# Scratch in DRAM laid out anew: token numbers 64 bytes apart, rows of x of 2112 bytes, rows of columns 320 bytes longer

## The chip, the core and the metric

The kernel runs on one core of a Trainium2 chip. The metric is the device time of one execution in microseconds. A core has five engines that run side by side, each with its own queue of instructions: TensorE (PE, with its weight loads as PEld), VectorE (DVE), ScalarE (ACT), GpSimd (POOL) and SyncE (SP), which here issues most DMAs. DMAs of all queues run on the core's 16 DMA engines, and the profile lists the fetches of the engines' own instructions among them, as queues of kind "instruction".

## The reference, cut to what matters

Three layers over 3072 tokens (4 sequences of 768) of 512 values:

```
scores = q @ k.T / 8; keep the first 4 keys and the last 128;  a = softmax(scores);  x = a @ v     # 8 heads of 64
logits = x @ w_gate + bias[modality];  e = argmax(logits);  gate = softmax(logits)[e]              # 8 experts
y[token] = gate * (relu(x[token] @ w1[e]) @ w2[e])                                                 # one expert a token
h = y @ w_in;  out = (h * sigmoid(1.702 * h)) @ w_out                                              # 512 -> 2048 -> 512
```

All inputs are float32. Which tokens an expert has is known on the chip only, so tokens are sorted there: rows of x go to DRAM, are gathered by expert, and the result goes to the right rows of the output at the end.

## The kernel before

**Attention** (up to about 240 us) runs over 24 tiles of 128 tokens; the order of its steps is a table of due times. At the end of each tile `norm` (L313 to L321) writes 128 rows of x to the scratch `xd`: the row of a token has 512 values and, behind them, one more place for its gate weight, 513 floats or 2052 bytes in all. The gate weights are made by `gate` (L791) in two batches, for tiles 0 to 15 while attention runs (L803 to L806) and for tiles 16 to 23 during routing: a sum, an addition, a reciprocal, and a DMA that puts one 4-byte word into each row. The DMA issues stand on SP's queue in the program's order.

**Routing** (about 244 to 262 us, mostly VectorE) sorts the tokens by expert and leaves lists of token numbers in `perm`, 128 to a column. One expert is chosen early from the first 2048 tokens, and its first pair of tiles is worked on while the rest is routed.

**Expert stage.** A pair is two tiles of 128 tokens of one expert (`pair`, and for the first one the loop over `ADV`). For each, POOL gathers the rows of x with their weights into the two tiles `xg` by an indirect DMA (`gather`, L1039), ACT multiplies by the weight (`weigh`, L1139), PE transposes, and then for eight chunks f of the hidden layer PE does 12 up-matmuls (`up`, L1166) and 12 down-matmuls (`down_pair`, L1181); ACT and DVE split each result into two parts between them. `yout` (L1240) evicts the pair's result into `ys` (L1245 on ACT and L1247 on DVE), columns by token, and `columns` (L1234) issues two DMAs for each place:

```
q.dma_start(out=m["y" + nm][:, :, bass.ds(at, n)]..., in_=ys[:, :, 0:n])      # L1237: 4 x 128 rows of n columns
q.dma_start(out=m["t" + nm][bass.ds(at, n)]..., in_=perm[:, j : j + n // P])   # L1238: the n token numbers
```

`yb` holds the columns of all tokens in sorted order (row pitch 12288 bytes), `ya` those of the first 1024 again (4096 bytes), and `tb` and `ta` their token numbers, 4 bytes each. The first pair goes to `ya`, the next three to `ya` and `yb`, the others to `yb`. Behind these DMAs on SP's queue stand weight chunks: of the next expert (`load_chunk`, L1095 and L1096), and of the last layer (`cload`, L1335 and L1337), which DVE and POOL convert. What is left over of an expert, up to 128 tokens, is done **alone** (`one`; up-matmuls L1478, down-matmuls L1487, loads under the branch of L1492): one tile, one matmul where a pair has three, weights read in place, and the next such expert's chunks are loaded as chunks come free; here POOL issues the y and token DMAs.

**Last layer** (from about 602 us). Twelve turns, two halves of the hidden layer by six groups of 512 tokens. `x2load` (L1468) reads the next group's columns and, in the second half, its token numbers into `oidx` (L1470) one turn ahead. The results are scattered to the output's rows by indirect DMAs (L1575).

Of the kernel before, what the change touches and what calls it, by code (L numbers as in the profile page):

```python
# [6 lines left out]
F32 = mybir.dt.float32  # L7
# [3 lines left out]
I32 = mybir.dt.int32  # L11
U32 = mybir.dt.uint32
AF = mybir.ActivationFunctionType
# [4 lines left out]
P = 128  # L18
B, H, S, D = 4, 8, 768, 64
NT = S // P  # L20
T = B * NT
E = 8
DM = H * D
# [767 lines left out]
def gate(tc, cst, pool, xd):  # L791

    nc = tc.nc
    V = nc.vector
    sm = pool.tile([P, T], F32, name="g_sm")
    d = cst["d"]

    def exps(a, b):
        V.tensor_tensor(out=d[:, a:b], in0=d[:, a:b], in1=cst["mx"][:, a:b].unsqueeze(2).broadcast_to([P, b - a, E]), op=ALU.subtract)
        nc.scalar.activation(out=d[:, a:b], in_=d[:, a:b], func=AF.Exp)  # L800

    def weights(a, b):
        V.tensor_reduce(out=sm[:, a:b], in_=d[:, a:b], op=ALU.add, axis=AX.X)  # L803
        V.tensor_scalar(out=sm[:, a:b], in0=sm[:, a:b], scalar1=1e-9, scalar2=None, op0=ALU.add)
        V.reciprocal(sm[:, a:b], sm[:, a:b])
        nc.sync.dma_start(out=xd[a * P : b * P, DM:].rearrange("(t p) o -> p (t o)", p=P), in_=sm[:, a:b])  # L806

    return exps, weights

# [200 lines left out]
NU = 16  # L1010
ADV = [(0, 7), (4, 8), (5, 1), (12, 0), (12, 2), (11, 5)]
F = 1024
CH = F // P
NG_ = T * P // 512


def whole(tc, q, k, v, n_sink, window, mid, wg, mb, w1, w2, w_in, w_out, out):
    nc = tc.nc
    w_in, w_out = w_in.bitcast(U32), w_out.bitcast(U32)
    with ExitStack() as ctx:  # L1020
        dp = ctx.enter_context(tc.tile_pool(name="dram", bufs=1, space=bass.MemoryType.DRAM))
        keep = ctx.enter_context(tc.tile_pool(name="keep", bufs=1))
        rp = ctx.enter_context(tc.tile_pool(name="raw", bufs=1))
        m = {}
        m["xd"] = dp.tile([T * P, DM + 1], F32, name="xd")

        for nm, n in (("a", 8 * P), ("b", T * P)):
            m["y" + nm] = dp.tile([4, P, n], F32, name="y" + nm)
            m["t" + nm] = dp.tile([n, 1], I32, name="t" + nm)
        m["yp"] = dp.tile([T * P, DM], F32, name="yp")  # L1030
        raw = [rp.tile([P, F], F32, name=f"raw{i}") for i in range(CH)]
        perm = keep.tile([P, NC], I32, name="perm")
        gp = ctx.enter_context(tc.tile_pool(name="xg", bufs=1, side="right"))
        xg = [gp.tile([P, DM + 1], F32, name=f"xg{i}") for i in range(2)]

        def gather(i, j):

# [61 lines left out]
def layers(tc, cst, ctx, c1, m, raw, keep, perm, gates, xg, gather, load, w_in, w_out, out):  # L1099
# [5 lines left out]
    nc = tc.nc  # L1105
    V, A, G = nc.vector, nc.scalar, nc.gpsimd
# [6 lines left out]
    def parts(p, nm, a, b):  # L1113
        return [(p.tile([P, F], F32R, name=f"{nm}h{i}"), p.tile([P, F], F32R, name=f"{nm}l{i}")) for i in range(a, b)]

# [20 lines left out]
    def weigh(i):  # L1136

        x = xg[i][:, 0:DM]
        A.activation(out=x, in_=x, func=AF.Copy, scale=xg[i][:, DM:])  # L1139

    def gather_alone(s):

# [3 lines left out]
    def trans_alone(s):  # L1146

        x = xs[s % 2]
        A.activation(out=x[:, 0:DM], in_=x[:, 0:DM], func=AF.Copy, scale=x[:, DM:])
        trans([x[:, 0:DM]], [(x, k) for k in range(4)])  # L1150

    def xtrans(u, blocks=range(2)):
# [45 lines left out]
    while (what := (yield)) is not None:  # L1198
        n = int(what[-1]) if what[-1].isdigit() else 0
        if what == "scores":  # L1200
            rp = pool("x", side="right")
            xt += [(rp.tile([P, F], F32R, name=f"xh{i}"), rp.tile([P, F], F32R, name=f"xl{i}")) for i in range(2)]
            hx += [rp.tile([P, 512], F32R, name=f"h{i}") for i in range(3)]
# [30 lines left out]
    def columns(q, places, n, j):  # L1234

        for nm, at in places:
            q.dma_start(out=m["y" + nm][:, :, bass.ds(at, n)].rearrange("k p c -> p k c"), in_=ys[:, :, 0:n])  # L1237
            q.dma_start(out=m["t" + nm][bass.ds(at, n)].rearrange("(i p) o -> p (i o)", p=P), in_=perm[:, j : j + n // P])  # L1238

    def yout(u, q=nc.sync):  # L1240

# [39 lines left out]
    cd, wb, xs = [], [], []  # L1281
# [25 lines left out]
    def left3():  # L1307
        nonlocal ca, cw
        c1.close()
        rp = pool("cd", side="right")  # L1310
        cd.extend(rp.tile([P, 2 * DM], F32, name=f"cd{i}") for i in range(2))
        wb.extend(parts(pool("wb", side="right"), "wb", 0, CH))
        tp = pool("moe")
        ca = tp.tile([P, 512], U32, name="ca")
        cw = tp.tile([P, 512], F32, name="cw")
        tp = pool("xs", c3)
        xs.extend(tp.tile([P, DM + 1], F32, name=f"xs{i}") for i in range(2))
        fresh[0] = flag(1, 1, (ET.SP,))
        expert[2] = expert_of(0, 2)
        with tc.If(fresh[0] != 0):  # L1320
            for c in range(CH):
                load(expert[2], c)
        ahead(1)
        cload(0)
        cload(1)
# [136 lines left out]
    oidx = keep.tile([P, T], I32, name="oidx")  # L1462

    def x2load(g, index=False):

        nm, a = ("b", 512 * g - 256) if g else ("a", 0)
        for i, x in enumerate(cd):
            nc.sync.dma_start(out=x.rearrange("p (k c) -> p k c", k=2), in_=m["y" + nm][2 * i : 2 * i + 2, :, a : a + 512].rearrange("k p c -> p k c"))  # L1468
        if index:
            nc.sync.dma_start(out=oidx[:, 4 * g : 4 * g + 4], in_=m["t" + nm][a : a + 512].rearrange("(t p) o -> p (t o)", p=P))  # L1470


    def first_alone(s, f):
# [68 lines left out]
    tp = pool("mlp")  # L1542
# [98 lines left out]
```

## Time and profile before

| | |
|---|---|
| time, median of 3 runs | 1136.49 us (1130.78 to 1139.29) |
| the profiled execution's own time | 1139.11 us, its span 1137.5 us |
| busy: PE, PEld | 1082.0 us (95%), 916.0 us (81%) |
| busy: DVE, ACT, POOL | 553.5 us (49%), 418.1 us (37%), 242.8 us (21%) |
| mean granted clock of PE | 0.975 |
| DMA | 172115 packets, 108.49 MB, 95 GB/s mean |
| packets under 512 bytes | 118000 |

Busy time is a mean over stages with different limits. [...] A timeline row has the start, the duration in us, engine, line, operation, and in square brackets the idle time ahead with what ended it; "issue" means that the profile shows nothing that the engine waited for.

### The profile page before, as it was taken

The page shows a single profiled execution, that of the slowest core. Times are in us where ns is not written, and L with a number is a line of the kernel's source. Part 1 is how long each engine was busy: PE and PEld are TensorE (multiplying, and loading weights), DVE is VectorE, ACT ScalarE, POOL GpSimd, SP SyncE. Part 2 cuts the span into 40 slices and gives each one's busy share as a digit, 9 for nine tenths or more (in the row PEclk, how much of TensorE's full clock was granted, in tenths as well). Part 3 has the DMA queues.
Part 4 walks back from the last instruction along what each step waited for, and adds up shares of the span by engine and source line. Part 5 has one row for each costly group of instructions (what it writes and reads, how often), then busy time and mean ns, then how long its engine had stood idle before and what let it go on. Part 6 is the DMA issues. An engine that isn't in the chain of part 4 may idle for free. (4 is left out here: it accounts for less than half of the span.)

```text
span 1137.5 us, 18802 instructions
## 1 busy us (share of the span) xinstructions
PE 1082.0 (95%) x6625; PEld 916.0 (81%) x6625; DVE 553.5 (49%) x1385; ACT 418.1 (37%) x1026; POOL 242.8 (21%) x397
## 2 busy tenths in 40 slices
PE   7999999888999999999869999999999999999996
PEld 4676766578998999999867888888888888888885
DVE  3776677785544484522102566656533334234242
ACT  4887887643222342222112323323323222223221
POOL 2523131452332233211100222222210011011011
PEclk8999999988988999999979999999999999999999
DMA  6667677642777865435666313112023023033010
GB/s 119 130 114 134 127 118 108 147 78 62 125 90 100 195 129 104 57 57 162 106 166 179 111 41 126 45 67 75 2 74 111 10 102 112 1 111 136 13 38 37
DMA packets 172115, 108.49 MB, mean 95 GB/s; under 512 B 118000, under 2 KB 149744, under 8 KB 171984
## 3 DMA queue, kind: packets, MB, share of 16 engines
q1 hardware_dynamic: 167184, 91.43, 38.3%
q0 software_dynamic: 4800, 15.49, 4.3%
q8 instruction: 60, 0.98, 0.4%
q14 instruction: 71, 0.58, 0.2%
HBM read 79.61 MB, written 27.29 MB: 94 GB/s over the span
## 5 line engine op out<-in xcount | busy, mean ns | idle before, releaser
L1166 PE MATMUL pu<-xh,wah 128*128 128x256 f32 (+1 forms) x576 | 187.3, 325 | 0.0
L1166 PE MATMUL pu<-xh,wal 128*128 128x256 f32 (+1 forms) x576 | 185.8, 323 | 0.4 <-DVEq L1275 0.4
L1166 PE MATMUL pu<-xl,wah 128*128 128x256 f32 (+1 forms) x576 | 185.7, 322 | 0.0
L1551 DVE TENSOR_TENSOR raw<-pu,raw 128x512 f32<-128x512 f32 x96 | 66.3, 691 | 244.8 <-ACT raw L1550 210.4
L1550 ACT ACTIVATE raw<-pu 128x512 f32<-128x512 f32 x96 | 57.4, 598 | 291.9 <-PE pu L1166 286.8
L1181 PE MATMUL pa<-h,wah 128*128 128x256 f32 x768 | 158.4, 288 | 5.1 <-issue 5.1
L1181 PEld LDWEIGHTS pa<-h,wah 128*128 128x128 f32 x768 | 130.3, 197 | 4.1 <-issue 4.1
L1166 PEld LDWEIGHTS pu<-xh,wal 128*128 128x128 f32 x576 | 112.2, 195 | 8.4 <-DVEq L1275 0.6
L1166 PEld LDWEIGHTS pu<-xh,wah 128*128 128x128 f32 x576 | 112.2, 195 | 8.3 <-issue 0.4
L1166 PEld LDWEIGHTS pu<-xl,wah 128*128 128x128 f32 x576 | 112.1, 195 | 7.5
L1181 PE MATMUL pa<-h,wal 128*128 128x256 f32 x384 | 110.6, 288 | 1.9 <-issue 1.9
L1189 ACT ACTIVATE h<-pu 128x256 fp32r<-128x256 f32 x96 | 36.9, 384 | 200.0 <-PE pu L1166 177.0
L1192 DVE SCALAR_TENSOR_TENSOR h<-pu,h 128x256 fp32r<-128x256 f32 x96 | 40.5, 422 | 125.2 <-ACT h L1189 64.5
L202 DVE CUSTOM_DVE_ANT_0 sc<-s,m 128x260 f32<-128x260 f32 (+1 forms) x192 | 73.1, 399 | 52.8 <-PE s L194 46.9
L211 ACT ACTIVATE pn<-sc,mx 128x260 f32<-128x260 f32 (+1 forms) x192 | 92.0, 483 | 5.2 <-DVE mx L202 4.7
L1118 ACT ACTIVATE h<-raw 128x512 fp32r<-128x512 f32 x96 | 60.7, 632 | 77.7 <-DVE raw L1551 77.7
L1181 PEld LDWEIGHTS pa<-h,wal 128*128 128x128 f32 x384 | 75.8, 197 | 3.4 <-issue 3.4
L1173 PE MATMUL pa<-wah,h 128*128 128x512 f32 x216 | 76.3, 389 | 0.0
L1173 PE MATMUL pa<-wbh,h 128*128 128x512 f32 x216 | 76.3, 389 | 0.0
L1166 PE MATMUL pu<-xh,wbh 128*128 128x512 f32 x192 | 74.8, 390 | 1.0 <-ACT y L1489 1.0
L1166 PE MATMUL pu<-xh,wbl 128*128 128x512 f32 x192 | 74.8, 390 | 0.0
L1166 PE MATMUL pu<-xl,wbh 128*128 128x512 f32 x192 | 74.8, 390 | 0.0
(327 smaller groups left out, 2067.8 us busy)
## 6 DMA issues: line engine op xcount, KB each, us to landing
raw<-in_moe_w_dram SPq DMA_DIRECT2D x64, 256.0 KB
cd<-yb SPq DMA_DIRECT2D x20, 512.0 KB
xd<-xe SPq DMA_DIRECT2D x24, 256.0 KB
raw<-yp SPq DMA_DIRECT2D x12, 512.0 KB
qn<-in_q_dram SPq DMA_DIRECT2D x22, 256.0 KB
kn<-in_k_dram SPq DMA_DIRECT2D x22, 256.0 KB
vn<-in_v_dram SPq DMA_DIRECT2D x22, 256.0 KB
yb<-y SPq DMA_DIRECT2D x10, 512.0 KB
```

The source lines that it names most:

```text
L202: nc.vector.tensor_tensor_reduce(out=sc[:, :n], in0=ps[:, :n], in1=m[:, :n], scale=1.0, scalar=3.0e38, op0=ALU.add, op1=ALU.min, accum_out=mx)
L211: nc.scalar.activation(out=pn[t][:, h, :n], in_=sc[:, :n], func=AF.Exp, scale=-1.0, bias=mx, accum_out=sums[t][:, h : h + 1])
L1118: A.activation(out=hi, in_=x, func=AF.Copy)
L1166: nc.tensor.matmul(ps[:, 0:n], w[a][:, s], cols(x, b, k), start=(k == 0 and i == 0), stop=(k == 3 and i == 2))
L1173: nc.tensor.matmul(acc, h[a][:, s], w[b][:, 512:], start=(f == 0 and j == 0), stop=(f == last and j == 2))
L1181: nc.tensor.matmul(acc[:, i % 2 * 256 : i % 2 * 256 + 256], wa[f][a][:, s], h[b], start=(f == 0 and i % 2 == 0 and j == 0), stop=(f == CH ...
L1189: A.activation(out=hi, in_=ps, func=AF.Relu)
L1192: V.scalar_tensor_tensor(out=lo, in0=ps, scalar=0.0, in1=hi.bitcast(F32), op0=ALU.max, op1=ALU.subtract)
L1550: A.activation(out=s, in_=ps, func=AF.Sigmoid, scale=1.702)
L1551: V.tensor_tensor(out=s, in0=ps, in1=s, op=ALU.mult)
```

## The change

`xd` gets rows of 528 floats (2112 bytes, 33 times 64), and the tiles that rows are gathered into (`xg`, `xs`) grow alike. The reciprocal writes each weight 16 times, into a new tile `g_sl`, and the DMA puts all 16 (64 bytes) behind the 512 values; the readers use the first. `ta` and `tb` have 16 places of 4 bytes for each token, of which the first is written and read. The rows of `ya` and `yb` are 80 floats (320 bytes) longer than their columns. No arithmetic changes.

```diff
--- before.py
+++ after.py
@@ -793,6 +793,7 @@
     nc = tc.nc
     V = nc.vector
     sm = pool.tile([P, T], F32, name="g_sm")
+    sl = pool.tile([P, T, LINE], F32, name="g_sl")
     d = cst["d"]
 
     def exps(a, b):
@@ -802,8 +803,8 @@
     def weights(a, b):
         V.tensor_reduce(out=sm[:, a:b], in_=d[:, a:b], op=ALU.add, axis=AX.X)
         V.tensor_scalar(out=sm[:, a:b], in0=sm[:, a:b], scalar1=1e-9, scalar2=None, op0=ALU.add)
-        V.reciprocal(sm[:, a:b], sm[:, a:b])
-        nc.sync.dma_start(out=xd[a * P : b * P, DM:].rearrange("(t p) o -> p (t o)", p=P), in_=sm[:, a:b])
+        V.reciprocal(sl[:, a:b], sm[:, a:b].unsqueeze(2).broadcast_to([P, b - a, LINE]))
+        nc.sync.dma_start(out=xd[a * P : b * P, DM:].rearrange("(t p) o -> p t o", p=P), in_=sl[:, a:b])
 
     return exps, weights
 
@@ -1010,6 +1011,9 @@
 NU = 16
 ADV = [(0, 7), (4, 8), (5, 1), (12, 0), (12, 2), (11, 5)]
 F = 1024
+LINE = 16
+PAD = 5 * LINE
+XD = DM + LINE
 CH = F // P
 NG_ = T * P // 512
 
@@ -1022,16 +1026,16 @@
         keep = ctx.enter_context(tc.tile_pool(name="keep", bufs=1))
         rp = ctx.enter_context(tc.tile_pool(name="raw", bufs=1))
         m = {}
-        m["xd"] = dp.tile([T * P, DM + 1], F32, name="xd")
+        m["xd"] = dp.tile([T * P, XD], F32, name="xd")
 
         for nm, n in (("a", 8 * P), ("b", T * P)):
-            m["y" + nm] = dp.tile([4, P, n], F32, name="y" + nm)
-            m["t" + nm] = dp.tile([n, 1], I32, name="t" + nm)
+            m["y" + nm] = dp.tile([4, P, n + PAD], F32, name="y" + nm)
+            m["t" + nm] = dp.tile([n, LINE], I32, name="t" + nm)
         m["yp"] = dp.tile([T * P, DM], F32, name="yp")
         raw = [rp.tile([P, F], F32, name=f"raw{i}") for i in range(CH)]
         perm = keep.tile([P, NC], I32, name="perm")
         gp = ctx.enter_context(tc.tile_pool(name="xg", bufs=1, side="right"))
-        xg = [gp.tile([P, DM + 1], F32, name=f"xg{i}") for i in range(2)]
+        xg = [gp.tile([P, XD], F32, name=f"xg{i}") for i in range(2)]
 
         def gather(i, j):
 
@@ -1136,7 +1140,7 @@
     def weigh(i):
 
         x = xg[i][:, 0:DM]
-        A.activation(out=x, in_=x, func=AF.Copy, scale=xg[i][:, DM:])
+        A.activation(out=x, in_=x, func=AF.Copy, scale=xg[i][:, DM : DM + 1])
 
     def gather_alone(s):
 
@@ -1146,7 +1150,7 @@
     def trans_alone(s):
 
         x = xs[s % 2]
-        A.activation(out=x[:, 0:DM], in_=x[:, 0:DM], func=AF.Copy, scale=x[:, DM:])
+        A.activation(out=x[:, 0:DM], in_=x[:, 0:DM], func=AF.Copy, scale=x[:, DM : DM + 1])
         trans([x[:, 0:DM]], [(x, k) for k in range(4)])
 
     def xtrans(u, blocks=range(2)):
@@ -1235,7 +1239,7 @@
 
         for nm, at in places:
             q.dma_start(out=m["y" + nm][:, :, bass.ds(at, n)].rearrange("k p c -> p k c"), in_=ys[:, :, 0:n])
-            q.dma_start(out=m["t" + nm][bass.ds(at, n)].rearrange("(i p) o -> p (i o)", p=P), in_=perm[:, j : j + n // P])
+            q.dma_start(out=m["t" + nm][bass.ds(at, n), 0:1].rearrange("(i p) o -> p (i o)", p=P), in_=perm[:, j : j + n // P])
 
     def yout(u, q=nc.sync):
 
@@ -1314,7 +1318,7 @@
         ca = tp.tile([P, 512], U32, name="ca")
         cw = tp.tile([P, 512], F32, name="cw")
         tp = pool("xs", c3)
-        xs.extend(tp.tile([P, DM + 1], F32, name=f"xs{i}") for i in range(2))
+        xs.extend(tp.tile([P, XD], F32, name=f"xs{i}") for i in range(2))
         fresh[0] = flag(1, 1, (ET.SP,))
         expert[2] = expert_of(0, 2)
         with tc.If(fresh[0] != 0):
@@ -1467,7 +1471,7 @@
         for i, x in enumerate(cd):
             nc.sync.dma_start(out=x.rearrange("p (k c) -> p k c", k=2), in_=m["y" + nm][2 * i : 2 * i + 2, :, a : a + 512].rearrange("k p c -> p k c"))
         if index:
-            nc.sync.dma_start(out=oidx[:, 4 * g : 4 * g + 4], in_=m["t" + nm][a : a + 512].rearrange("(t p) o -> p (t o)", p=P))
+            nc.sync.dma_start(out=oidx[:, 4 * g : 4 * g + 4], in_=m["t" + nm][a : a + 512, 0:1].rearrange("(t p) o -> p (t o)", p=P))
 
 
     def first_alone(s, f):
```

On VectorE's queue one instruction has another size in each batch of weights. In the second batch, in the routing, there stood before (the names are the tiles, `r_` those of the routing):

```order
L803 TENSOR_REDUCE g_sm<-pk_d 128x8
L804 TENSOR_SCALAR g_sm<-g_sm 128x8
L805 RECIPROCAL g_sm<-g_sm 128x8
L860 TENSOR_SCALAR r_pn<-r_n 128x8
L862 TENSOR_SCALAR r_pn<-r_pn 128x8
```

and now stands:

```order
L804 TENSOR_REDUCE g_sm<-pk_d 128x8
L805 TENSOR_SCALAR g_sm<-g_sm 128x8
L806 RECIPROCAL g_sl<-g_sm 128x128
L861 TENSOR_SCALAR r_pn<-r_n 128x8
L863 TENSOR_SCALAR r_pn<-r_pn 128x8
```

Nothing moved; the reciprocal has 128 values a partition in place of 8, and 256 in place of 16 in the first batch.

On SP's queue, the DMAs of a pair's result with the computation of their places, before (pair 2, counted from 0):

```order
L1237 REGISTER_ALU
L1237 DMA yb<-y 128x4x256
L1238 REGISTER_ALU
L1238 DMA tb<-perm 128x2x1
L1237 REGISTER_ALU
L1237 DMA ya<-y 128x4x256
L1238 REGISTER_ALU
L1238 DMA ta<-perm 128x2x1
```

and now:

```order
L1241 REGISTER_ALU
L1241 DMA yb<-y 128x4x256
L1242 ISA
L1242 DMA tb<-perm 128x2x1
L1241 REGISTER_ALU
L1241 DMA ya<-y 128x4x256
L1242 ISA
L1242 DMA ta<-perm 128x2x1
```

The DMAs are as many and in the same order; ahead of a token write another instruction computes its place. In later pairs one such instruction is added.

## Rows read from the trace of the kernel before

**Rows 1.** The page, its first part, and PE in its 40 slices.

```profile
PE 1082.0 (95%) x6625; PEld 916.0 (81%) x6625; DVE 553.5 (49%) x1385; ACT 418.1 (37%) x1026; POOL 242.8 (21%) x397
...
PE   7999999888999999999869999999999999999996
```

**Rows 2.** Windows between evictions of y; pair 1 first; columns named above.

```profile
core 0: us, PE busy (x) PEld busy (x) DVE busy (x) ACT busy (x) POOL busy (x), PEclk, DMA share, GB/s
297.99:328.62 30.63, 26.33 (x202) 26.23 (x201) 12.25 (x27) 5.97 (x13) 9.02 (x9) 0.89 0.69 96
328.62:359.01 30.39, 27.78 (x206) 27.04 (x205) 11.96 (x26) 7.30 (x15) 9.04 (x9) 0.89 0.73 96
359.01:387.62 28.61, 26.37 (x206) 25.98 (x205) 11.96 (x26) 7.30 (x16) 8.00 (x8) 0.94 1.03 152
387.62:411.53 23.91, 23.91 (x202) 23.91 (x201) 18.75 (x30) 11.89 (x19) 9.64 (x8) 1.00 0.73 195
```

**Rows 3.** Timeline of SP: the token write of a later pair.

```profile
437.62 0.39 SPq L1238 DMA_DIRECT2D tb<-perm  x1
```

**Rows 4.** Windows of 1 us behind that token write.

```profile
439.00:440.00 1.00, 1.00 (x11) 1.00 (x10) 0.00 (x0) 0.21 (x1) 0.91 (x2) 1.00 0.65 177
...
442.00:443.00 1.00, 1.00 (x11) 1.00 (x10) 0.01 (x1) 0.64 (x2) 0.00 (x0) 1.00 0.00 0
...
445.00:446.00 1.00, 1.00 (x11) 1.00 (x10) 0.90 (x3) 0.00 (x0) 0.80 (x1) 1.00 1.05 45
...
449.00:450.00 1.00, 1.00 (x11) 1.00 (x10) 0.93 (x3) 0.00 (x1) 0.00 (x0) 1.00 0.96 349
```

**Rows 5.** Window of 1 us in pair 0's write of y.

```profile
274.00:275.00 1.00, 1.00 (x11) 1.00 (x10) 0.97 (x8) 0.42 (x2) 0.00 (x0) 1.00 0.99 336
```

**Rows 6.** Timeline of PE in pair 2, first and last of three gaps.

```profile
312.85 0.28 PE L1181 MATMUL pa<-h,wah 128*128 128x256 f32 x1 [2.15 <-issue]
...
315.64 0.37 PE L1181 MATMUL pa<-h,wah 128*128 128x256 f32 x1 [1.03 <-issue]
```

**Rows 7.** DMA queues (packets, MB, share) in 197:201, 245:248, 252:254.

```profile
q8 instruction: 1, 0.02, 9.2%
...
q1 hardware_dynamic: 1040, 0.00, 15.6%
...
q8 instruction: 1, 0.02, 2.7%
```

**Rows 8.** Windows in the stretch of experts that run alone.

```profile
554.00:602.00 48.00, 34.20 (x260) 33.04 (x260) 2.92 (x5) 8.61 (x24) 3.99 (x5) 0.86 0.65 134
...
562.00:563.00 1.00, 1.00 (x11) 1.00 (x10) 0.00 (x0) 0.28 (x1) 0.00 (x0) 1.00 1.12 12
...
587.00:588.00 1.00, 0.00 (x0) 0.00 (x0) 0.00 (x0) 0.30 (x1) 0.00 (x0) 1.00 0.17 27
```

**Rows 9.** Timeline of PE in that stretch, its two longest gaps.

```profile
572.31 1.01 PE L1478 MATMUL pu<-xs,raw 128*128 128x128 f32 x3 [5.34 <-DMA raw<-in_moe_w_dram]
...
592.37 1.01 PE L1478 MATMUL pu<-xs,raw 128*128 128x128 f32 x3 [5.76 <-SPq L1492]
```

**Rows 10.** Chain that ended last (start, us, what): one chunk at full clock.

```profile
596.15 1.09 PE pu L1478 x8
597.24 0.89 PE pa L1487 x8
```

**Rows 11.** The tile of gate weights: reciprocals and DMAs (duration ns min/median/max).

```profile
L805 DVE RECIPROCAL g_sm<-g_sm x2: 202/228/253, 193.1 to 245.5; 128x16 f32<-128x16 f32 x1, 128x8 f32<-128x8 f32 x1
L806 SPq DMA_DIRECT2D xd<-g_sm x2: 382/386/389, 193.4 to 245.7; - x2
```

**Rows 12.** Timeline of PE in the opening: waits for the first gathered tiles.

```profile
226.25 0.33 PE L1130 MATMUL pu<-ident,xg 128*128 128x128 f32 x1 [2.74 <-ACT xg L1139]
...
228.25 1.75 PE L1130 MATMUL pu<-ident,xg 128*128 128x128 f32 x7 [1.67 <-ACT xg L1139]
```

**Rows 13.** Window in the routing.

```profile
249.00:252.00 3.00, 3.00 (x27) 3.00 (x27) 3.00 (x11) 1.34 (x2) 1.46 (x2) 1.00 0.00 0
```

## The prediction

> **What bounds the kernel now.** I read the page's first part, then the windows stage by stage, and only then single instructions. TensorE is busy for 1082.0 of 1137.5 us [rows 1], so no engine beside it can give much; what a change of memory layout can give lies in the 55 us in which TensorE stands still and in the time its clock is lowered after standing still. The windows by pair of the expert stage show where that is [rows 2]: from one eviction of y to the next a pair of 256 tokens takes 30.63, 30.39 and 28.61 us three times running, and 23.91 us in the fourth. The matmuls are the same (202, and 206 in two, where four transposes are added), but the granted clock is 0.89, 0.89 and 0.94 in place of 1.00 and TensorE is not busy all the time. The 23.91 is what the work costs; the rest is stall.
>
> Why it stalls is seen one level down. After each eviction the kernel issues y and then the token numbers: for the later pair shown, 128x2 words of 4 bytes to adjacent places at 437.62 [rows 3]. By the microsecond [rows 4], the queue moves 177 GB/s in the slice in which these words go (439 to 440), then 0 in 442 to 443 and 45 in 445 to 446, with a weight chunk waiting behind them, and 349 again from 449 on: about 9 us of jam behind 1 KB. It isn't y that jams: in 274 to 275, while the last of pair 0's y goes and a gather beside it, the rate is 336 GB/s [rows 5]. In the three slow pairs y and the numbers go out twice, to two places, and there TensorE stops in the middle of an accumulation, matmul by matmul, with no releaser (three gaps; the first and the last of them in [rows 6]): nothing but its next instructions can be late, and these come over the same DMA engines (a code packet of 0.02 MB takes 9.2% of 16 engines over 4 us, which is 5.9 us, when it meets short writes, and 2.7% over 2 us, 0.9 us, when it does not [rows 7]). [...]
>
> The second place is the stretch of the experts that run alone: 48 us for 260 matmuls, clock 0.86 [rows 8], with gaps of 5.34 and 5.76 us before matmuls that wait for weights [rows 9]. The rate falls to 12 and 27 GB/s in it [rows 8], behind token writes again. The rest, from 602 us to the end, is steady matmul work with its x2 and index loads a whole turn ahead; nothing in the change reaches it.
>
> **The change part by part.**
>
> *Token numbers 64 bytes apart.* As many writes of 4 bytes, no two within 64 bytes. Is the jam made by their number or by their adjacency? The trace holds the other case: the gate weights, 4 bytes each and 2052 bytes apart. Their 2048 words are issued at 193.4 [rows 11], and the code packet of the window from 197 on takes its 5.9 us, to 203 [rows 7]: about 9 us for 2048, 4.4 ns each. The second batch (1040 packets after 245.7) is gone when a code packet of 0.9 us passes after 252 [rows 7]: under 5 us, at most 5 ns each. The adjacent 256 cost 9 us, 35 ns each. So adjacency costs eight times, and 256 apart should cost 256 x 5 ns, some 1.3 us. Ends: 0 and 9 us a batch; I take 1.3, the row of like instructions. The worth, then:
> - Pairs: 6.72 + (6.48 - 0.5) + (4.70 - 0.5) = 16.9 us over 23.91 [rows 2], the 0.5 for the four transposes that two of them add (four at the 0.12 us a matmul of these rows). A jam of 2.6 us for two batches is shorter than the 9 us that the later pairs ride out without loss. I take 16.0; ends 0 and 16.9.
> - Experts alone: eight up-matmuls take 1.09 and eight down-matmuls 0.89 us at full clock [rows 10], so two experts of eight chunks take 2 x 8 x 1.98 = 31.7, with the transposes 32.2; the stretch took 48, so 15.8 is stall and low clock. What is late next is the weights themselves: 4 MB an expert, which at the 177 to 349 GB/s outside the jam of rows 4 needs 12 to 24 us, beside 16 us of matmuls. So I leave some 3 us of it: 12.5; ends 0 and 15.8.
>
> *Rows of x from 64-byte places, weight 16 times.* A row was 2052 bytes, so its 256-byte pieces began 4 bytes further on in each row; now 2112. The gathers move 3% more. Where they matter is the opening: TensorE waits 2.74 and 1.67 us for two gathered tiles, 4.4 in all [rows 12], issued right beside a write of x. With the edges of the pieces whole, the write should clear sooner. That is inferred, not shown; ends 0 and 4.4, I take 3.0. In the attention stage the same writes stand among the loads, but TensorE's slices read 9 there from the second on [rows 1], with no idle time to give back, so I cost it at nothing; its cover is the two-tile lead of the loads.
>
> *The reciprocal.* It now writes 256 and 128 values in place of 16 and 8. 16 took 0.25 and 8 took 0.20 us [rows 11]: 6.4 ns a value, so 256 take 1.79 and 128 take 0.97: +1.5 and +0.8. The second lies where VectorE is busy throughout (3.00 of 3 us [rows 13]) and everything waits for the routing: its 0.8 counts in full. The first lies in attention, where VectorE has gaps: ends 0 and 1.5, I take 0.7. Together +1.5. The gathers that need the weights come long after.
>
> *Rows of columns 320 bytes longer.* y already goes at 336 GB/s [rows 5]; nothing to gain, and its reads are ahead of need. Zero; a cost would be hidden by the turn of lead. The instruction that replaces a register operation on SP ahead of a token write, and one added in later pairs, stand in a queue that waits for y anyway: zero.
>
> Sum against the profiled execution's 1139.1 us: -16.0 - 12.5 - 3.0 + 1.5 = -30.0, so **1109 us**. That execution lies 2.6 us above the median of 1136.49, and the runs spread over 8.5 us; since stalls are what I remove, I count from the execution that shows them.
>
> [...] In the rows, 4-byte writes 2052 bytes apart cost an eighth of adjacent ones. [...] The weights in rows 7 and the tokens in rows 4, of one length and two spacings, speak against length alone, but no row shows 64 bytes.
>
> **The rivals.**
> - *The short write itself is the cost (no change).* Every 4-byte write would still be slow, and 64 bytes too little distance: the unit that serialises may be wider, or the 16 KB that 256 tokens now cover may still meet at one place. Then the jams stay at 9 us and only the reciprocals count: 1139.1 + 1.5, down to 1136 where rows of x help: 1136 to 1142. For it: no row has a spacing between 4 and 2052 bytes. Against: whatever the unit's width, sixteen times fewer tokens share one. 12%.
> - *The jam goes, the stall half stays.* The pairs run free, but the lone experts become bound by their weight loads, or code still comes late in one pair: half of 28.5 is given back, 1117 to 1128. For it: in that stretch the loads are issued only as chunks come free. Against: a chunk comes free three chunks after its use, five before its place is read again, which is 5 x 1.98 = 10 us of lead. 9%.
> - *The other side: each place costs what 64 bytes cost now.* 256 tokens fill 16 pieces of 64 bytes and take 9 us, 0.56 us a piece. If the piece is what costs, and not the words in it, 256 pieces cost more than now. It decides from where a jam is longer than the 9 us that the later pairs ride out; at 18 us the eight later pairs would lose what the first three lose, 5.6 on average, and the lone stretch 9 twice: 1139 + 45 + 18 = 1202 us, and more for longer jams. Against: 2048 weights, each in a piece of its own, cleared in 9 us [rows 7]. 5%.
>
> **How the numbers follow.** The forecast holds 74%: 1100 to 1117, from the ends of its terms (-16.9 - 15.8 - 4.4 + 0.8 gives 1103, and a little for stalls too small for a row; half the lone stretch kept and nothing from the opening gives 1117). With the half case up to 1128 the range **1100 to 1128** leaves out the other two cases and a little at its edges, 2 in 10. A measurement can't tell less than about 1% from no change, 11 us, so faster means below 1125: the forecast and most of the half case, 0.80; within 1%: no change and the rest of it, 0.14; slower 0.06.
>
> **What would show it.** Right: all pairs at 23.9 to 24.5 us with clock 1.00; over 200 GB/s within 2 us of a token write wherever something is queued behind it; the stretch of lone experts at 34 to 37 us; the gaps without a releaser gone; reciprocals of about 1.8 and 1.0 us. Wrong: the rate falls to tens of GB/s for 8 us behind the tokens as before (no change), or for longer (slower); weight waits of several us among lone experts with no jam ahead of them (half). If the gathers of the opening still end late while the tokens run free, the term of 3.0 was wrong and the rest stands.

## The result, and the profile after

The changed kernel takes **1103.47 us** (median of 4 runs, 1102.95 to 1104.96), the kernel before in the same comparison 1135.45 us (4 runs, 1130.78 to 1139.29): ratio 0.9729, 95% interval 0.9699 to 0.9758. The forecast was 1109 us, 1100 to 1128. The profiled execution took 1102.95 us (span 1101.4), 36.2 us less than the one the prediction counted from.

In what follows a line of the changed kernel has a number one to four higher than before: the up-matmuls are L1170, the y and token DMAs L1241 and L1242.

The first part of the page, and PE in its 40 slices:

```profile
PE 1068.0 (97%) x6625; PEld 904.5 (82%) x6625; DVE 553.7 (50%) x1385; ACT 418.2 (38%) x1026; POOL 241.9 (22%) x397
...
PE   6999999978999999999989999999999999999996
```

As many matmuls, 14 us less busy time (fewer of them at half clock, PEclk 0.50, as before from 343.9 to 350.7 us; the mean granted clock is 0.989, against 0.975), and of 36 us in all the rest is time in which TensorE stood still. The windows between evictions of y, with the columns of [rows 2], show where (in brackets the number of instructions; PEclk is the granted clock of PE as a share of full speed; the DMA share, of the 16 DMA engines, can pass 1 in a short window, since a packet's whole time is put where it began); the last row is the stretch of the experts that run alone, from the last pair's eviction to the last lone one's:

```profile
294.67:318.58 23.91, 23.91 (x202) 23.91 (x201) 11.95 (x26) 5.97 (x14) 8.98 (x9) 1.00 0.40 124
318.58:343.00 24.42, 24.42 (x206) 24.34 (x205) 11.95 (x26) 7.29 (x15) 8.99 (x9) 1.00 0.39 120
343.00:367.54 24.54, 24.54 (x206) 24.37 (x205) 11.96 (x26) 7.30 (x16) 7.95 (x8) 1.00 0.77 238
367.54:391.45 23.91, 23.91 (x202) 23.91 (x201) 18.75 (x30) 11.88 (x19) 9.60 (x8) 1.00 0.42 134
532.06:565.24 33.18, 30.38 (x266) 29.63 (x264) 3.46 (x5) 9.21 (x25) 3.99 (x5) 1.00 0.66 195
```

The three doubled pairs take what the fourth always took; the four added transposes are the 0.5 us that was allowed for. Between the same evictions the lone stretch took 48.65 us before. The whole difference by the times of the evictions of y:

| stretch | before | after | difference | forecast |
|---|---|---|---|---|
| start to pair 0's y | 270.00 | 266.92 | -3.08 | -3.0 + 1.5, opening and reciprocals |
| first pair after it | 27.99 | 27.75 | -0.24 | 0 |
| three doubled pairs | 89.64 | 72.87 | -16.77 | -16.0 |
| later pairs | 165.11 | 164.52 | -0.59 | 0 |
| lone experts | 48.65 | 33.18 | -15.47 | -12.5 |
| last layer (to TensorE's end) | 526.46 | 526.47 | 0.01 | 0 |

For the jam itself, SP's issues of a later pair's y, numbers and next weight chunk in the timeline (to be held against [rows 3]):

```profile
440.81 0.40 SPq L1241 DMA_DIRECT2D yb<-y  x1
441.46 0.39 SPq L1242 DMA_DIRECT2D tb<-perm  x1
443.66 0.36 SPq L1341 DMA_DIRECT2D cd<-in_moe_w_out_dram  x1
```

and the windows of 1 us behind them, with the columns of [rows 2] (against [rows 4]):

```profile
443.00:444.00 1.00, 1.00 (x11) 1.00 (x10) 0.00 (x0) 0.08 (x1) 0.91 (x2) 1.00 0.42 100
444.00:445.00 1.00, 1.00 (x11) 1.00 (x10) 0.28 (x1) 0.38 (x1) 0.92 (x2) 1.00 0.27 94
445.00:446.00 1.00, 1.00 (x11) 1.00 (x11) 0.14 (x1) 0.00 (x0) 0.71 (x1) 1.00 1.02 389
446.00:447.00 1.00, 1.00 (x11) 1.00 (x10) 0.19 (x1) 0.82 (x2) 0.00 (x0) 1.00 0.16 57
```

The numbers go at 443.2, and the chunk behind them is through at 446.3, at 389 GB/s in the third slice. A window with 0 GB/s is by itself no jam, though: once the chunk is through nothing is queued, and 447 to 448 reads 0 here too. The measure used below is therefore the time from the start of the first number's packet to the start of the last of the chunk's 128 packets of 4096 bytes: 10.4 and 10.6 us in two later pairs before, 3.6 and 3.1 us in the same two now.

### The profile page after: what moved, and what is told of

The parts are those of the page before. It is cut to its first block, busy times and chain, and to the rows that moved or that the text cites. A ratio compares the mean times of both kernels' runs of the same rounds, so it can differ in the third digit from the quotient of the medians.

```text
span 1101.4 us, 18806 instructions
## 1 busy us (share of the span) xinstructions
PE 1068.0 (97%) x6625; PEld 904.5 (82%) x6625; DVE 553.7 (50%) x1385; ACT 418.2 (38%) x1026; POOL 241.9 (22%) x397
## 5 line engine op out<-in xcount | busy, mean ns | idle before, releaser
L1170 PE MATMUL pu<-xh,wah 128*128 128x256 f32 (+1 forms) x576 | 185.6, 322 | 0.0
L1170 PE MATMUL pu<-xh,wal 128*128 128x256 f32 (+1 forms) x576 | 184.2, 320 | 0.4 <-DVEq L1279 0.4
L1170 PE MATMUL pu<-xl,wah 128*128 128x256 f32 (+1 forms) x576 | 184.2, 320 | 0.1
L1185 PE MATMUL pa<-h,wah 128*128 128x256 f32 x768 | 155.4, 286 | 0.0
L1185 PEld LDWEIGHTS pa<-h,wah 128*128 128x128 f32 x768 | 128.0, 194 | 0.0
L1170 PEld LDWEIGHTS pu<-xh,wal 128*128 128x128 f32 x576 | 110.4, 192 | 8.2 <-DVEq L1279 0.6
L1170 PEld LDWEIGHTS pu<-xh,wah 128*128 128x128 f32 x576 | 110.5, 192 | 7.8 <-ACTq L1279 0.2
L1170 PEld LDWEIGHTS pu<-xl,wah 128*128 128x128 f32 x576 | 110.3, 192 | 7.8 <-DVE xl L1123 0.3
L1170 PE MATMUL pu<-xh,wbh 128*128 128x512 f32 x192 | 74.8, 390 | 1.2 <-ACT y L1493 1.2
L1170 PE MATMUL pu<-xh,wbl 128*128 128x512 f32 x192 | 74.7, 389 | 0.0
L1170 PE MATMUL pu<-xl,wbh 128*128 128x512 f32 x192 | 74.7, 389 | 0.0
```

Source lines behind the costliest of these rows:

```text
L1170: nc.tensor.matmul(ps[:, 0:n], w[a][:, s], cols(x, b, k), start=(k == 0 and i == 0), stop=(k == 3 and i == 2))
L1185: nc.tensor.matmul(acc[:, i % 2 * 256 : i % 2 * 256 + 256], wa[f][a][:, s], h[b], start=(f == 0 and i % 2 == 0 and j == 0), stop=(f == CH ...
```

## The experiments

Twelve kernels ran, in four groups; each group had its own runs of the kernel before, whose medians were 1131.57, 1133.53, 1131.33 and 1140.48 us. Ratios are against those.

**1. The tokens alone** (kernel before; the token DMAs, L1238 and L1470, then write and read the first of the 16 places):

```diff
-            m["t" + nm] = dp.tile([n, 1], I32, name="t" + nm)
+            m["t" + nm] = dp.tile([n, 16], I32, name="t" + nm)
```

> The kernel before with one part of the change alone: token numbers 64 bytes apart. If the adjacent 4-byte writes make the jams, the three slow pairs fall to 23.9 to 24.5 us and the stretch of lone experts to about 33 us, while y(0) stays where it was, near 270: 1137.5 - 16.8 - 15.5 - 0.5 gives a span of 1104 to 1106. If it is the pitch of y's rows (a power of two, or three times one) that jams the writes, nothing moves: 1134 to 1140. If both are needed, something between.

Measured 1106.76 us (1105.23 to 1109.32), ratio 0.9792 (0.9766 to 0.9819). The doubled pairs take 23.90, 24.42 and 24.52, the lone stretch 33.28:

```profile
534.23:567.51 33.28, 30.37 (x266) 29.62 (x264) 3.46 (x5) 9.02 (x24) 3.99 (x5) 1.00 0.63 194
```

So the tokens alone bring both large terms, without the new rows of x and the 16 weights. The opening's two waits are still there (1.15 and 3.00 us).

**2. All but the tokens** (changed kernel, with the tokens side by side again):

```diff
-            m["t" + nm] = dp.tile([n, LINE], I32, name="t" + nm)
+            m["t" + nm] = dp.tile([n, 1], I32, name="t" + nm)
```

> The changed kernel with the tokens put back side by side: rows of x of 2112 bytes, weights 16 times, and the longer rows of columns remain. By the adjacency theory the jams stay, three slow pairs of 28 to 31 us and a lone stretch of 46 to 49 us, and only the opening is gained: y(0) near 267 and a time of 1130 to 1136. By the pitch theory the jams go and the time is about 1105 to 1108.

Measured 1119.87 us (1116.73 to 1125.89), ratio 0.9908 (0.9876 to 0.9940): the time expected was missed by over 10 us. The jams are there, but in the traced execution the doubled pairs lose 1.8 us and not 16.8:

```profile
294.68:318.59 23.91, 23.91 (x202) 23.91 (x201) 12.22 (x27) 5.97 (x14) 8.99 (x9) 1.00 0.99 108
318.59:344.82 26.23, 24.55 (x206) 24.34 (x205) 12.25 (x26) 7.29 (x15) 8.96 (x9) 1.00 0.89 127
344.82:369.34 24.52, 24.52 (x206) 24.35 (x205) 12.05 (x26) 7.29 (x15) 7.96 (x8) 1.00 0.99 103
536.06:578.73 42.67, 33.70 (x266) 32.38 (x264) 3.46 (x5) 8.90 (x24) 3.99 (x5) 0.92 0.70 152
```

TensorE's code packet of this pair is served at 315.2, against 302.6 in the changed kernel, and TensorE doesn't stop. (The packets of queue q8, 16384 bytes each, are taken for TensorE's code because they keep step with its work: in the last layer of the changed kernel it runs 226 to 286 matmuls and weight loads from one packet to the next, 256 on average.) With that the prediction's reason for the pairs' stall, late code, came into doubt, and the runs from 5 on were made for it.

**3. Without the 320 bytes** (changed kernel):

```diff
-PAD = 5 * LINE
+PAD = 0
```

> The changed kernel without the 320 bytes at the end of each row of columns. If the pad does nothing, 1102 to 1106, pairs of 23.9 to 24.5 us, lone stretch 33 us, as in the changed kernel. If rows of columns at a power of two jam as well, part of the stalls is back: over 1110.

1103.56 us (1102.18 to 1104.38), ratio 0.9752 (0.9728 to 0.9777), pairs and lone stretch as in the changed kernel. The longer rows do nothing.

**4. The short reciprocal** (changed kernel, the 16 copies made by GpSimd):

```diff
-        V.reciprocal(sl[:, a:b], sm[:, a:b].unsqueeze(2).broadcast_to([P, b - a, LINE]))
+        V.reciprocal(sm[:, a:b], sm[:, a:b])
+        nc.gpsimd.tensor_copy(sl[:, a:b], sm[:, a:b].unsqueeze(2).broadcast_to([P, b - a, LINE]))
```

> The changed kernel with the reciprocal of 16 and 8 values as before, and GpSimd copying each 16 times. If the long reciprocal costs the path what it takes, 1.5 us in the first and 0.75 us in the second batch, y(0) comes 0.75 to 2.2 us earlier than 266.9 and the time is 1101 to 1103. If the reciprocals lie beside other work, or GpSimd's copy slows VectorE as much, y(0) stays at 266.5 to 267.5 and the time within 1 us of 1103.5.

1102.09 us (1102.00 to 1105.82), ratio 0.9743 (0.9720 to 0.9767): not to be told from the changed kernel. Pair 0's y comes at 267.06, against 266.92 there, so the second expectation is met on that point.

**5 and 6. Which part made run 2 faster: the longer rows of columns alone, and the new rows of x alone** (kernel before; the texts name 79.7 us for the doubled pairs of run 2, by a slip: the trace gives 74.7, from 294.68 to 369.34). The first edit, and of the second the two lines that set the layout (its readers change with them, as in the diff of the change):

```diff
-            m["y" + nm] = dp.tile([4, P, n], F32, name="y" + nm)
+            m["y" + nm] = dp.tile([4, P, n + 80], F32, name="y" + nm)
```

```diff
-        m["xd"] = dp.tile([T * P, DM + 1], F32, name="xd")
+        m["xd"] = dp.tile([T * P, XD], F32, name="xd")
...
-        V.reciprocal(sm[:, a:b], sm[:, a:b])
+        V.reciprocal(sl[:, a:b], sm[:, a:b].unsqueeze(2).broadcast_to([P, b - a, LINE]))
```

> The kernel before with nothing changed but the rows of columns 320 bytes longer; tokens side by side, rows of x of 2052 bytes. With tokens side by side, the longer rows of columns and the new rows of x took three quarters of the loss out of the three doubled pairs (79.7 us for them, against 89.6 before and 72.9 after the change), and this run and the next tell which of the two did it. Theory that the rows of x did it (a gather of 256-byte pieces that begin 4 bytes further on in each row is slower while the tokens jam the queue): no difference from the kernel before, ratio 0.997 to 1.003, the three pairs at 88 to 91 us, gaps of TensorE without a releaser in all three. Rival, that the pitch of the rows of columns did it (4096 and 12288 bytes before, 4416 and 12608 now): the three pairs at 78 to 82 us and a ratio of 0.990 to 0.994.

> The kernel before with nothing changed but the rows of x (2112 bytes, the weight 16 times); tokens side by side, rows of columns as before. If the rows of x took the loss out of the doubled pairs in the run with all but the tokens changed: the three pairs at 78 to 82 us, the opening about 3 us shorter, ratio 0.988 to 0.994. Rival, that the pitch of the rows of columns did it: the three pairs at 88 to 91 us, the opening about 3 us shorter all the same, ratio 0.996 to 0.999.

Longer rows alone: 1136.69 us, ratio 1.0026 (1.0002 to 1.0050), doubled pairs 92.1 us in all: no gain. Rows of x alone: 1127.78 us (1121.36 to 1133.99), ratio 0.9950 (0.9917 to 0.9983), doubled pairs 84.0 us, of which one is free:

```profile
297.25:325.51 28.26, 25.88 (x202) 25.58 (x201) 12.50 (x28) 6.00 (x13) 8.98 (x9) 0.94 0.90 108
325.51:356.72 31.21, 27.09 (x206) 26.89 (x205) 11.97 (x26) 7.31 (x16) 8.98 (x9) 0.89 0.71 94
356.72:381.25 24.53, 24.53 (x206) 24.36 (x205) 11.97 (x26) 7.32 (x16) 7.96 (x8) 1.00 1.08 166
```

The longer rows have no part in run 2's gain, and the rows of x have one, but less than was expected of them; what makes up the rest isn't shown, and each trace is of one execution. With tokens side by side a kernel's runs also spread over 4 to 13 us, with tokens apart over 4 at most: whether a pair stalls is partly chance.

**7. Tokens 16 bytes apart** (changed kernel, 4 places for each token in place of 16):

```diff
-            m["t" + nm] = dp.tile([n, LINE], I32, name="t" + nm)
+            m["t" + nm] = dp.tile([n, 4], I32, name="t" + nm)
```

> The changed kernel with the tokens 16 bytes apart, four to 64 bytes, in place of one. Theory that what costs is writes that fall within the same 64 bytes: a quarter of the sharing is left, a jam of some 9 / 4 = 2.3 us a batch, which the pairs ride out: the three pairs at 73 to 74 us, the lone stretch at 33 to 36, 1103 to 1107 us. Rival, that anything within 64 bytes is as bad as side by side: the jams at 8 to 9 us as with the tokens side by side, 1116 to 1122 us. Rival, that the distance alone matters little and the 16 KB over which 64-byte places spread is what helps: between the two, 1108 to 1115.

1103.41 us (two runs, 1101.94 and 1104.88), ratio 0.9739 (0.9677 to 0.9801), pairs 23.91, 24.43 and 24.53, lone stretch 33.61. The chunk behind the numbers is through in 3.8 us, against 3.3 at 64 bytes: half a microsecond is left of the jam where 2.3 were expected.

**8. One place for the numbers** (kernel before; `ta` is filled at the start with numbers out of range, and the output rows that would be taken from it are left out):

```diff
-            q.dma_start(out=m["t" + nm][bass.ds(at, n)].rearrange("(i p) o -> p (i o)", p=P), in_=perm[:, j : j + n // P])
+            if nm == "b" or len(places) == 1:
+                q.dma_start(out=m["t" + nm][bass.ds(at, n)].rearrange("(i p) o -> p (i o)", p=P), in_=perm[:, j : j + n // P])
```

> The kernel before with the token numbers of pairs 1 to 3 written to one place (the sorted list) and not to the list of the first 1024 as well, which is filled with numbers out of range ahead of time; so the output rows that are taken from that list for these pairs are left out. y still goes to both places. Theory that the second batch makes the jam longer than a pair rides out: the three pairs fall to 73 to 75 us, no gap of TensorE without a releaser in them, the lone stretch stays at 46 to 49 us, 15 to 17 us under the kernel before. Rival, that one batch beside two writes of y is enough to stall TensorE: the three pairs at 80 to 90 us.

1127.63 us (1124.23 to 1130.48), ratio 0.9948 (0.9924 to 0.9972): the three pairs take 81.8 us, so the first expectation is missed. But the three are not alike:

```profile
295.73:319.63 23.90, 23.90 (x202) 23.90 (x201) 12.25 (x27) 5.99 (x14) 8.98 (x9) 1.00 0.68 123
319.63:348.71 29.08, 26.03 (x206) 25.82 (x205) 11.96 (x26) 7.31 (x15) 8.97 (x9) 0.94 0.61 100
348.71:377.55 28.84, 26.00 (x206) 25.80 (x205) 11.97 (x26) 7.33 (x16) 7.97 (x8) 0.94 0.93 199
```

What tells them apart is the order on SP's queue. The first of them goes to `ya` and then to `yb`, the others to `yb` first; with the numbers of `ta` gone, the first pair has no numbers between its two copies of y, and the others still have:

```profile
297.21 0.38 SPq L1240 DMA_DIRECT2D ya<-y  x1
297.64 0.50 SPq L1240 DMA_DIRECT2D yb<-y  x1
298.19 1.05 SPq L1242 DMA_DIRECT2D tb<-perm  x1
...
321.19 0.40 SPq L1240 DMA_DIRECT2D yb<-y  x1
321.83 0.40 SPq L1242 DMA_DIRECT2D tb<-perm  x1
322.45 0.72 SPq L1240 DMA_DIRECT2D ya<-y  x1
```

The packets of y (1024 bytes) take at most 88 ns in the first, and up to 2.8 and 3.2 us in the others. The timeline of TensorE in the second pair shows how it stalls (L1169 are the up-matmuls, L1184 the down-matmuls, L1133 transposes for a lone expert):

```profile
330.96 0.28 PE L1169 MATMUL pu<-xl,wah 128*128 128x256 f32 x1
331.08 0.28 PE L1184 MATMUL pa<-h,wah 128*128 128x256 f32 x1
...
332.40 0.28 PE L1184 MATMUL pa<-h,wah 128*128 128x256 f32 x1
335.74 0.66 PE L1133 MATMUL pt<-ident,xs 128*128 128x128 f32 x4 [3.05 <-ACT xs L1152]
```

and that of ScalarE what it waited for (L1192 evicts the up-matmuls' result, L1152 scales the rows of x that are transposed):

```profile
334.46 0.39 ACT L1192 ACTIVATE h<-pu 128x256 fp32r<-128x256 f32 x1 [5.67 <-remote]
334.96 0.72 ACT L1152 ACTIVATE xs<-xs 128x512 f32<-128x512 f32 x1
```

The chunk's last up-matmul ends at 331.24. In the changed kernel ScalarE takes its result at once (330.24, the matmul having ended at 330.20); here it starts at 334.46, 3.2 us late, released by a count of TensorE's semaphore ("remote": by nothing that ended just then). TensorE's next count, due at 332.7, comes at 334.56, and between 334.38 and 334.75 the 16 DMA engines report the end of a transfer. So a signal between two engines came late, and TensorE, which needs the transposes behind it, waited for ScalarE.

**9. Tokens 8 bytes apart** (changed kernel, 2 places for each token):

```diff
-            m["t" + nm] = dp.tile([n, LINE], I32, name="t" + nm)
+            m["t" + nm] = dp.tile([n, 2], I32, name="t" + nm)
```

> The changed kernel with the tokens 8 bytes apart, eight to 64 bytes. What is read is the weight chunk queued right behind the tokens of a later pair (128 packets of 4096 bytes): its packets start within 10 us with tokens side by side, within 3 us at 64 bytes and within 3.5 us at 16. Theory that the cost goes by how many tokens fall within the same 64 bytes: half of the jam is left, the chunk within 6 to 8 us, 1104 to 1110 us. Rival, that only words that lie side by side cost: the chunk within 3 to 4 us as at 16 bytes, 1102 to 1106 us.

1107.10 us (1106.36 and 1107.84), ratio 0.9781 (0.9749 to 0.9812); the pairs are free, the lone stretch takes 36.6 us. The chunk is through in 5.2 us, between the two expectations. Over the 3.3 us at 64 bytes that leaves 7.2, 1.9 and 0.5 us with 16, 8 and 4 numbers to 64 bytes: about a quarter for each halving, steeper than the sharing itself.

**10. The numbers twice in the later pairs** (kernel before; a second batch to an unread array, behind the first):

```diff
+            if len(places) == 1 and nm == "b":
+                q.dma_start(out=m["tc"][bass.ds(at, n)].rearrange("(i p) o -> p (i o)", p=P), in_=perm[:, j : j + n // P])
```

> The kernel before, with the token numbers of each pair that has one place, and of each lone expert, written a second time to a spare array that nobody reads, side by side as well. Theory that one batch is ridden out and two behind each other hold up the engines' counts and the code until TensorE stops: the later pairs go from 23.9 to 26 to 31 us each, as the three doubled pairs did before, and the lone stretch grows beyond 49 us; 1150 to 1190 us in all. Rival, that it takes the second writing of y, or what stands around it in the first pairs: the later pairs stay at 23.9 us, and the total within 1% of the kernel before, apart from the lone stretch.

1132.03 us (1130.53 to 1134.20), ratio 1.0010 (0.9994 to 1.0026): the first expectation fell, by 18 us and more. Most later pairs don't notice:

```profile
402.80:426.69 23.89, 23.89 (x202) 23.89 (x201) 16.72 (x32) 7.75 (x15) 8.20 (x8) 1.00 0.60 113
426.69:450.60 23.91, 23.91 (x202) 23.91 (x201) 11.83 (x26) 5.98 (x14) 7.97 (x8) 1.00 0.59 90
```

The lone stretch takes 46.3 us, no longer than before. Nor is the jam much longer: the chunk is through in 10.9 and 11.2 us, against 10.4 and 10.6 with half the numbers. So the jam isn't so much a write; two arrays jam together in little more than the time of one.

The next three pairs take 24.0, 24.3 and 23.9 us, but the last takes 26.52, where the kernel before took 21.63. TensorE stops in it in the middle of an accumulation; the third row is TensorE's code packet, from the DMA queues in the window from 541 to 544:

```profile
522.79:549.31 26.52, 23.09 (x178) 22.92 (x177) 4.70 (x10) 5.21 (x12) 2.00 (x2) 0.91 0.46 116
...
545.04 0.55 PE L1182 MATMUL pa<-h,wah 128*128 128x256 f32 x1 [3.43 <-issue]
...
q8 instruction: 1, 0.02, 3.4%
```

Here code is late. The packet takes 3.4% of 16 engines over 3 us, 1.6 us, from 541.89 to 543.50, behind the last of the weights that stood behind the numbers (541.14), and TensorE goes on 1.5 us after it has landed. The last pair has this stop, before the same matmul and always 1.5 to 1.6 us after the packet has landed, in six of the seven kernels with tokens side by side (0.33 us in the kernel before, 1.81 in run 12, 0.1 to 0.9 in the other three), and in none of the seven with tokens 8 bytes or more apart. Whether the doubled numbers made it longer here isn't shown.

**11. Four times the numbers, 64 bytes apart** (changed kernel; each batch also to three unread arrays):

```diff
+            for c in range(3):
+                q.dma_start(out=m["t" + nm + str(c)][bass.ds(at, n), 0:1].rearrange("(i p) o -> p (i o)", p=P), in_=perm[:, j : j + n // P])
```

> The changed kernel with every batch of token numbers written four times, 64 bytes apart, three of them to spare arrays that nobody reads: 1024 writes of 4 bytes a place, 2048 in the doubled pairs, four times as many as before the change. Theory that the number of short writes costs little and the side by side did it: at most 5 ns a write, some 4 us more behind each place, which a pair rides out: pairs at 23.9 to 24.6 us and 1102 to 1112 us. Rival, that the number of short writes counts (a jam of 1024 at 35 ns would be 36 us): the pairs stall again, 1130 us and more.

1105.06 us (1104.95 and 1105.16), ratio 0.9763 (0.9734 to 0.9791), pairs 23.91, 24.42 and 24.51. The chunk is through in 4.4 and 3.9 us: 0.85 us for 768 more writes, 1.1 ns each.

**12. Both copies of y ahead of the numbers** (kernel before, one line added, so that the DMAs of a doubled pair go y, y, numbers, numbers):

```diff
         for nm, at in places:
             q.dma_start(out=m["y" + nm][:, :, bass.ds(at, n)]..., in_=ys[:, :, 0:n])
+        for nm, at in places:
             q.dma_start(out=m["t" + nm][bass.ds(at, n)]..., in_=perm[:, j : j + n // P])
```

> The kernel before with one change of order: in the doubled pairs both copies of y are issued first and both batches of token numbers behind them (before: y, numbers, y, numbers). Tokens side by side, as many writes and bytes as before. Theory, from the runs with one place and with the numbers twice: side by side numbers stall TensorE where the second copy of y is queued behind them, and not by themselves: the three doubled pairs fall from 82 to 90 us to 73 to 76, no packet of y takes longer than 0.6 us in them, the lone stretch stays at 42 to 49 us, ratio 0.984 to 0.990. Rival, that two batches of numbers within 2 us are too much wherever they stand: the three pairs at 81 to 90 us, ratio 0.996 to 1.004.

1124.45 us (1118.75 to 1129.57), ratio 0.9885 (0.9844 to 0.9926), as the theory had it. The traced execution is the fastest of the four; whether the three pairs run free in the others isn't shown. The windows of the three pairs and of the lone stretch:

```profile
296.95:320.85 23.90, 23.90 (x202) 23.90 (x201) 12.88 (x28) 5.98 (x13) 9.21 (x10) 1.00 0.78 132
320.85:345.27 24.42, 24.42 (x206) 24.34 (x205) 11.96 (x26) 7.19 (x15) 9.02 (x9) 1.00 0.72 119
345.27:369.79 24.52, 24.52 (x206) 24.35 (x205) 11.96 (x26) 7.30 (x15) 8.00 (x8) 1.00 0.87 159
...
536.48:580.67 44.19, 33.15 (x266) 32.02 (x264) 3.46 (x5) 8.91 (x25) 4.00 (x5) 0.88 0.62 146
```

and windows of 1 us behind the numbers of the first of these pairs:

```profile
304.00:305.00 1.00, 1.00 (x11) 1.00 (x10) 0.50 (x1) 0.96 (x2) 0.06 (x1) 1.00 0.00 0
305.00:306.00 1.00, 1.00 (x10) 1.00 (x10) 0.79 (x2) 0.27 (x1) 0.99 (x1) 1.00 0.00 0
...
311.00:312.00 1.00, 1.00 (x10) 1.00 (x10) 0.32 (x2) 0.38 (x1) 0.63 (x1) 1.00 0.49 25
```

The jam is as long as ever (12.4 us from the first number to the end of the chunk), and TensorE runs through it. Of the DMA queues in the window from 303 to 311 (packets, MB, share), the one that was read in [rows 7]:

```profile
q8 instruction: 1, 0.02, 5.4%
```

5.4% of 16 engines over 8 us is 6.9 us for TensorE's code packet, from 303.7 on, longer than the 5.9 in [rows 7]; and TensorE doesn't miss a beat in this pair. In the three pairs no packet of y takes longer than 0.14 us.

## Why the prediction was right, and where its reason was not

**That spacing the numbers takes the jam away** held: 10.5 us to 3.3 from the first number to the end of the chunk behind, and the run with the tokens alone gives both large terms. Of the two ways to price it, number or adjacency, run 11 shows number to be nearly free (0.85 us for 768 more) and runs 7 and 9 adjacency to be what costs (3.8 us with 4 numbers to 64 bytes, 5.2 with 8, 10.5 with 16). The price of the side by side case, 35 ns a write times their count, is wrong in form: run 10 doubles the count for some 0.6 us. The other price, 5 ns a write for 256 numbers 64 bytes apart, was too high: not 1.3 us, but by run 11 256 x 1.1 ns, 0.3 us. Run 11, with its 1024 writes of 4 bytes a place and the chunk through in 4.4 and 3.9 us, shows that the length is not what costs here.

**Pairs, -16.0; measured -16.8.** The term held and its reason did not; its size was read from [rows 2], and only asked that the stall go with the jam. The failed step is "nothing but its next instructions can be late": run 12 has the jam and a code packet of 6.9 us, and no stall; run 2 passes the place with the packet 12.6 us late; and in the kernel before TensorE goes on at 312.85 [rows 6], when its packet hasn't begun (313.24). So late code isn't what stops TensorE in the doubled pairs; how far ahead of its use code is fetched isn't shown. In the last pair, where TensorE goes on 1.5 to 1.6 us after a packet has landed in six kernels (run 10), the prediction's reason is the right one, for the half microsecond that the last pair gained.

What the stall of the doubled pairs needs is the order y, numbers, y, numbers: the second copy of y is written from behind the jam. Take the numbers from between the copies (run 12; the first pair of run 8) and the loss is gone with the jam in full; put as many numbers where no y follows (run 10) and most pairs lose nothing, the last one to late code. The order isn't enough by itself: run 2 has it in all three pairs, with packets of y that take up to 4.3, 7.3 and 3.9 us, and two of the three run free. The rows to read were SP's issues in the doubled pairs, which the prediction never listed; it saw that these pairs write twice and left it at that. From the timeline of the kernel before:

```profile
299.47 0.38 SPq L1237 DMA_DIRECT2D ya<-y  x1
299.90 0.50 SPq L1238 DMA_DIRECT2D ta<-perm  x1
300.45 0.98 SPq L1237 DMA_DIRECT2D yb<-y  x1
301.48 0.57 SPq L1238 DMA_DIRECT2D tb<-perm  x1
```

It also overlooked that in the second and third of the slow stretches the last gap ends before transposes that wait for ScalarE, as in run 8 (0.91 and 1.61 us); and that in the first [rows 6] ScalarE waits too, released as in run 8, in the same microsecond in which TensorE is free again:

```profile
315.84 0.39 ACT L1189 ACTIVATE h<-pu 128x256 fp32r<-128x256 f32 x1 [8.67 <-remote]
```

**How** a write stuck in the jam holds up a count between engines, and TensorE in the middle of its matmuls, stays open; so does why runs 2 and 6, with the new rows of x, lose less to it.

**Lone experts, -12.5; measured -15.5.** The mechanism held: the weights were queued behind the numbers. Runs with tokens side by side take 42.7 to 48.7 us there, in whatever order y goes (44.2 in run 12), and those with tokens 16 or 64 bytes apart 33.2 to 34.2. It isn't the weights alone that come late: in run 12 TensorE's longest wait there, 7.58 us, is for ScalarE, which waits for the last layer's columns, whose read was issued 1.2 us after the numbers. The size was off: 3 us were left for weights as the next thing to be late, and what is left is a gap of 1.69 us and one of 0.84. The floor of 32.2 us that the prediction worked out was the better figure.

**Opening, -3.0, and reciprocals, +1.5; together measured -3.1.** TensorE's two waits [rows 12] became one of 1.63 us. Over all runs pair 0's y comes at 267.6 us on average with the new rows of x (8 kernels, 266.9 to 268.5) and at 269.4 with the old (6 kernels, 268.0 to 271.0): some 1.9 us net, so of the 3.1 part is chance. Rows and copies of the weight changed together in all eight, so which of them gained it isn't shown. The prediction also read 9 for TensorE in all of the attention stage from its second slice on; [rows 1] has 8 from 199 us (a slice is 28.4 us), where these waits lie. The reciprocals took what was forecast, 1.75 and 0.95 us, and run 4 shows nothing of it on the path, so the +1.5 was put too high as far as one execution tells:

```profile
L806 DVE RECIPROCAL g_sl<-g_sm x2: 952/1352/1752, 193.3 to 242.5; 128x256 f32<-128x256 f32 x1, 128x128 f32<-128x128 f32 x1
```

**The 320 bytes, and SP's instructions, 0:** run 3 (1103.56 us without the bytes, 1103.47 with them) and the later pairs (164.52 us in all, 165.11 before) agree.

Of the 6.2 us between the sum (1109) and the profiled execution (1102.95), the lone experts make 3.0, the opening and the first pair with the reciprocals 1.8, the doubled pairs 0.8 and the last pair 0.5. Of the rivals, the half-kept stall needed weight loads that bind the lone experts, and they don't; the short write as the cost by itself is refuted by run 1, the slow 64-byte piece by run 11.

No version beat the changed kernel: those of runs 3, 4 and 7 are equal to it within a few tenths of a per cent, and the one added line of run 12 gets 1.15% where the change gets 2.7%.

## What to carry to other kernels

Look for short writes side by side in DRAM, a list of indices for instance, and ask what is queued behind them: here a weight chunk behind 256 of them was through in 10.5 us in place of 3.3, and with a second copy of y behind them ScalarE started 3.2 us late (run 8). Space the words (16 bytes sufficed here, 3.8 us in run 7), or where the layout is fixed issue the long writes first (1.15% in run 12). When a stall has no releaser, don't name its cause by exclusion; list the issues of every queue ahead of it, in a case that stalls and in one that doesn't, and see whether the engine goes on when the late thing lands or before.

## What the runs showed that was not expected

- Jam behind 256 words of 4 bytes: 7.2 us with 16 of them to 64 bytes, 1.9 with 8, 0.5 with 4; 512 words in two arrays, little more than 256 in one (11.1 against 10.5 us with the chunk); 1024 words 64 bytes apart, under 1 us more than 256.
- A count from TensorE to ScalarE reached it 3.2 us after the matmul that carried it, in a jam (run 8), against 0.04 us outside.
- A code packet that takes 6.9 us, or is served 12.6 us late, costs TensorE nothing in a doubled pair (runs 12 and 2); in the last pair it stands still until 1.5 us after its packet has landed, up to 3.43 us (run 10).
